# Attention and a snake MLP in one kernel: w_out's last row blocks ahead of v, two requests for late weight pieces, and a new order at the seam of the first two tiles

## The chip, the cores and the metric

One core of a Trainium2 chip runs the whole kernel in one launch. The metric is the device time of one execution in microseconds, the median of several runs. A profile of one further execution shows what each engine did: TensorE (PE; its weight loads are PEld), VectorE (DVE), ScalarE (ACT), GpSimd (POOL), SyncE (SP, which here only issues transfers) and the 16 DMA engines.

## The reference

```python
# q, k, v: 8 batches x 8 heads x 576 rows x 64, f32
q_s = exp(q - max(q, axis=-1));  q_s /= sum(q_s, axis=-1)      # over the 64 columns of a row
k_s = exp(k - max(k, axis=2));   k_s /= sum(k_s, axis=2)       # over the 576 rows
kv   = einsum('bhsd,bhse->bhde', k_s, v)                       # 64 x 64 per head
attn = einsum('bhsd,bhde->bhse', q_s, kv)
x = attn.transpose(0, 2, 1, 3).reshape(4608, 512)
h = x @ w_in                                                   # 512 -> 2048
s = sin(alpha * h)
g = h + s * s / alpha
out = g @ w_out                                                # 2048 -> 512, f32
```

## The kernel before

**Tiles.** The 4608 tokens are nine tiles of 512. For each tile the first product is 16 slots (`ni`) of 128 columns of w_in. A slot is four matmuls of 128x512 (`mm_h`, L275 to L284), one for each chunk of 128 of the 512 inputs, taken in the order 0, 2, 1, 3 (`KO`). ScalarE takes the sine out of PSUM (`sine`, L286), one of ScalarE, GpSimd and VectorE squares it, VectorE combines it with h into g in bf16 (`combine`, L297). The second product is, for each of four blocks of 128 tokens (called m or j), 16 matmuls over the row blocks `ni` of w_out (`mm_o`, L301); its accumulator is copied out of PSUM and stored by two transfers (`evac_o`, L311).

**Attention.** exp of q and k on ScalarE, the row sums and the norm of q on VectorE, v cast to bf16 with a column of ones beside it, so that k's sum falls out of the same product. For batches 0 and 1, `wide_mm(b, ii)` (L178) multiplies k and v for one half of the heads with 18 matmuls, and `wide_norm` (L187) scales the result into `kvw`; `attn_x` (L232) multiplies it with q transposed, and copies put the result into `xT`: half 0 gives the chunks 0 and 2, half 1 the chunks 1 and 3. `ii` is the half throughout.

**Order.** The schedule is written by hand: each engine runs its instructions in the order of the program and waits where one needs another's result. Each of two queues carries loads: SP's (`nc.sync`) takes q, k, v and the stores; GpSimd's takes w_in and w_out, whose requests cast from f32 to bf16 on the way.

**The start.** Batch 0's attention is done first, with w_in coming in pieces (L358 to L363, the last of 512 columns, slots 12 to 15) and w_out's row blocks 0 to 7 behind it (L364). Tile 0's slots run at L478; the dictionary `late` (L476) issues loads after certain slots: q of batch 1 (`load_q1`, L460), w_out's blocks 8 to 11 after slot 8 and 12 and 13 after slot 10, k and v of batch 1 after slot 12 (`load_kv1`, L468). Row blocks 14 and 15 come as f32 on SP's queue into two buffers (`late_w`, L488) behind batch 1's v, and are cast at L543 by GpSimd and ScalarE. Behind them on that queue are `q8` (the ninth row of each group of q for batches 0 and 1, L491) and batch 2's q, k and v.

**The seam of tiles 0 and 1.** Tile 0's second product is a generator of 64 matmuls (`o_quad`, L439): four runs of 16, each over four row blocks of w_out and all four m. The main program takes some of them at a time (`take(os, n)`) between the steps of batch 1's attention: 42, then the first set of transposes of q, 9, the second set, 1, the first wide kv, 3, the first half of attention, 1, the second wide kv, the first products of tile 1's slots 0 and 1 (chunks 0 and 2), the second half of attention, and the last 8. Each accumulator is evacuated as soon as its last product is issued. The four accumulators are in the PSUM buffers "b", "b", "l", "l", and the slots of tile 1 take these over again as they are listed in `BANKS`.

Before tile 1's first sine, ScalarE has exp of `q8` (L545) and a small sine (L551) by which the Sin table is loaded. Tile 1's second product (`o_stream`, L591) takes its first two blocks of tokens up to `ni` 13 each before the last two `ni` of both.

Of the kernel before, what the change touches and what calls it, by code (L numbers as in the profile page):

```python
# [15 lines left out]
F32 = mybir.dt.float32  # L16
BF16 = mybir.dt.bfloat16
AX = mybir.ActivationFunctionType
# [5 lines left out]
def kernel(  # L24
# [14 lines left out]
    nc = tc.nc  # L39
# [7 lines left out]
    nN = d_ff // 128  # L47
    MF = 512
# [12 lines left out]
    spool = ctx.enter_context(tc.tile_pool(name="spool", bufs=4))  # L61
# [6 lines left out]
    xT = singles.tile([128, 4, NX], BF16, name="xT")  # L68
    q8 = singles.tile([128, 4, 2, D], F32, name="q8")
    win = singles.tile([128, 4, d_ff], BF16, name="win")  # L70
    wout = singles.tile([128, nN, dm], BF16, name="wout")
# [11 lines left out]
    wout_v = moe_w_out.rearrange("(no ni) d -> ni no d", ni=128)  # L83
# [23 lines left out]
    def load_win(c0, c1, cc=slice(0, 4)):  # L107
        nc.gpsimd.dma_start(out=win[:, cc, c0:c1], in_=win_v[:, cc, c0:c1])  # L108

    def load_wout(n0, n1):  # L110
        nc.gpsimd.dma_start(out=wout[:, n0:n1, :], in_=wout_v[:, n0:n1, :])
# [43 lines left out]
    def norm_q8():  # L155

        qe = A["qe", 1][:, J - 2:J].rearrange("p b (i d) -> p b i d", i=4)
        qs = small.tile([128, 2, 4], F32, name="qs8")
        nc.vector.tensor_reduce(qs, qe, axis=AXL.X, op=ALU.add)
        nc.vector.reciprocal(qs, qs)  # L160
        return lambda: nc.vector.tensor_tensor(qe, qe, qs.unsqueeze(3).to_broadcast([128, 2, 4, D]), op=ALU.mult)
# [101 lines left out]
    G = {}  # L263

    HP = {}
    BANKS = {0: "aabbkllaabbkllaa", 1: "aakbbllaabbllaab", 2: "aabbopaabbopaabb"}

    def bank(kind):

        if kind == "k":  # L270
            return ps_k.tile([128, 2, MF], F32, name="kvp", tag="a")[:, 0]
        pool = {"a": lambda: ps_h[0], "b": lambda: ps_h[1], "l": lambda: ps_l, "o": lambda: ps_o[0], "p": lambda: ps_o[1]}[kind]()
        return pool.tile([128, MF], F32, name={"l": "lp", "o": "op", "p": "op"}.get(kind, "hp"), tag=kind)

    def mm_h(t, ni, k0=0, k1=4):  # L275

        if ni == 0 and k0 == 0:
            G[t] = gpool.tile([128, nN, MF], BF16, name="g")
        hp = HP[t, ni] if k0 else bank(BANKS.get(t, 3 * "aabb" + "abba")[ni])
        HP[t, ni] = hp  # L280
        for k in range(k0, k1):
            nc.tensor.matmul(hp, win[:, KO[k], ni * 128:(ni + 1) * 128],  # L282
                             xT[:, KO[k], t * MF % NX:t * MF % NX + MF], start=(k == 0), stop=(k == 3))
        return hp  # L284

    def sine(t, ni, hp, sq):  # L286
        s = spool.tile([128, MF], F32, name="s")
        nc.scalar.activation(s, hp, AX.Sin, scale=alpha_sb[:, ni:ni + 1])  # L288
        if sq == "A":
            nc.scalar.activation(s, s, AX.Square)  # L290
        elif sq == "P":
            nc.gpsimd.tensor_tensor(s, s, s, op=ALU.mult)  # L292
        else:
            nc.vector.tensor_tensor(s, s, s, op=ALU.mult)
        return s
# [9 lines left out]
    def place(blk):  # L305

        if blk < 2 * (J - 1):
            return blk // (J - 1), blk % (J - 1)
        return (blk - 2 * (J - 1), J - 1) if blk < 2 * J else (blk // J, blk % J)

    def evac_o(t, j, acc, eng, cols=None, queues=None):  # L311
        cols = cols or slice(0, dm)
        o = opool.tile([128, dm], F32, name="o")
        eng(o[:, cols], acc)  # L314
        for hf in range(2):
            bb, jj = place(t * BPT + 2 * j + hf)
            (queues or (nc.sync, nc.sync))[hf].dma_start(out=out_v[bb, jj][:, cols],
                                                         in_=o[64 * hf:64 * hf + 64, cols])


    ACT_CP, DVE_CP, GP_CP = nc.scalar.copy, nc.vector.tensor_copy, nc.gpsimd.tensor_copy
# [13 lines left out]
    zero = singles.tile([128, 1], F32, name="zero")  # L335
# [24 lines left out]
    load_win(0, 512, slice(1, 4, 2))  # L360
    for c in range(2, 6):
        load_win(256 * c, 256 * c + 256)
    load_win(1536, 2048)  # L363
    for c in range(2):  # L364
        load_wout(4 * c, 4 * c + 4)

# [62 lines left out]
        mm_h(0, ni, ki, ki + 1)  # L429

    def h_slot(t, ni, sq, lag):
        hp = mm_h(t, ni, 2 if ni < (4, 2, 0)[min(t, 2)] else 0)
        lag.append((t, ni, hp, sine(t, ni, hp, sq)))

    def flush(lag, keep):
# [3 lines left out]
    def o_quad(t, accs, engs):  # L439

        R = range(4)
        by_m, by_n = [(n, m) for m in R for n in R], [(n, m) for n in R for m in R]
        orders = [by_m, by_n, by_n, by_n[:8] + [(n, m) for m in R for n in (2, 3)]]
        for c in R:
            for n, m in orders[c]:
                mm_o(t, m, 4 * c + n, accs[m])
                if c == 3 and n == 3:
                    evac_o(t, m, accs[m], engs[m])
                yield

    def take(it, n=1000):
        for _ in range(n):
            if next(it, 0) == 0:
                return
# [4 lines left out]
    with ES:  # L459
        def load_q1(ii):  # L460
            if ii == 0:
                staged["q", 1] = stage.tile([128, 4, J, D], F32, name="st_q", tag="st")
            st = staged["q", 1]
            DVE_CP(st[:, ii, 0, 0:1], zero)
            nc.sync.dma_start(out=st[:, ii::2, 0:8].rearrange("p i j d -> p i (j d)"),
                              in_=src_view(q, 1)[:, ii::2, 0:8 * D])

        def load_kv1():  # L468
            for n in "kv":
                staged[n, 1] = stage.tile([128, 4, J, D], F32, name=f"st_{n}", tag="st")  # L470
            for n, t, ii, j0, j1 in (("k", k, 0, 0, J), ("v", v, 0, 0, J), ("k", k, 1, 0, J),
                                     ("v", v, 1, 0, 5), ("v", v, 1, 5, J)):
                nc.sync.dma_start(out=staged[n, 1][:, ii::2, j0:j1].rearrange("p i j d -> p i (j d)"),
                                  in_=src_view(t, 1)[:, ii::2, j0 * D:j1 * D])

        late = {6: lambda: load_q1(0), 8: lambda: load_wout(8, 12), 10: lambda: load_wout(12, 14),  # L476
                12: lambda: (load_q1(1), load_kv1())}
        for ni in range(nN):  # L478
            h_slot(0, ni, "DPPAPPAPPAAPPAPD"[ni], lag)
            flush(lag, 1)  # L480
            if ni in late:
                late[ni]()
        flush(lag, 0)

        accs = [bank(kind) for kind in "bbll"]
        os = o_quad(0, accs, [DVE_CP, ACT_CP, DVE_CP, DVE_CP])

        late_w = [spool.tile([128, MF], F32, name="s") for _ in range(2)]  # L488
        for n in range(2):
            nc.sync.dma_start(out=late_w[n], in_=wout_v[:, 14 + n])  # L490
        for b in range(2):  # L491
            nc.sync.dma_start(out=q8[:, :, b], in_=src_view(q, b)[:, :, 8 * D:J * D])
        load_batch(2)
# [1 line left out]
        def cast_v1(ii):  # L495
            vv = vb[1].rearrange("p j (i c) -> p i j c", i=4)
            for j0, j1, eng in (((0, 5, ACT_CP), (5, 9, GP_CP)), ((0, 5, GP_CP), (5, 9, DVE_CP)))[ii]:
                eng(vv[:, 2 * ii:2 * ii + 2, j0:j1, 0:D], staged["v", 1][:, ii::2, j0:j1])
# [29 lines left out]
        exp_half("k", 1, 1)  # L528
        take(os, 9)
        transpose_q1(1, DVE_CP)  # L530
        take(os, 1)
        wide_mm(1, 0)
        wide_norm(1, 0)
        take(os, 3)
        cast_v1(1)
        xa = [bank("a") for _ in range(2)]
        attn_x(1, 0, 0, 8, xa)
        for x in range(2):
            (ACT_CP, DVE_CP)[x](xT[:, 2 * x, MF:2 * MF], xa[x])
        take(os, 1)  # L540
        wide_mm(1, 1)
        wide_norm(1, 1)
        for n, eng in ((0, GP_CP), (1, ACT_CP)):  # L543
            eng(wout[:, 14 + n], late_w[n])
        exp_to(A["qe", 1][:, J - 2:J], q8)  # L545
        for ni, ki in ((0, 0), (1, 0), (0, 1), (1, 1)):
            mm_h(1, ni, ki, ki + 1)
        xb = ps_k.tile([128, 2, MF], F32, name="kvp", tag="a")
        attn_x(1, 1, 0, 8, [xb[:, x] for x in range(2)])
        DVE_CP(xT[:, 1:4:2, MF:2 * MF], xb)  # L550
        nc.scalar.activation(zero, zero, AX.Sin)  # L551
        take(os)
        scale_q8 = norm_q8()
        load("q", q, 3)
        load("k", k, 3)
# [35 lines left out]
    def o_stream(t, eng=DVE_CP):  # L591
        order = [(j, ni) for j in range(4) for ni in range(nN)]
        if t == 1:
            order = [(j, ni) for n0, n1 in ((0, nN - 2), (nN - 2, nN)) for j in range(2) for ni in range(n0, n1)] + order[2 * nN:]
        acc = {}
        for j, ni in order:
            if ni == 0:
                acc[j] = bank("b" if t == 1 and j == 0 else "op"[j % 2])
            mm_o(t, j, ni, acc[j])
            if ni == nN - 1:  # L600
                evac_o(t, j, acc[j], eng)
            yield
# [4 lines left out]
    os = o_stream(1)  # L607
# [55 lines left out]
    for t in range(3, nT):  # L663
        b = t + 1 if t + 1 < B else None
        os = o_stream(t - 1)
# [9 lines left out]
        for ni in range(nN):  # L675
            hp = mm_h(t, ni)
# [20 lines left out]
            s = sine(t, ni, hp, "A")  # L697
# [41 lines left out]
```

## Time and profile before

| | |
|---|---|
| median of 3 runs | 281.84 us (281.73 to 281.9) |
| the profiled execution | 283.14 us, its span 281.3 us |
| granted TensorE clock in it | 0.999 |
| TensorE without a matmul, of the span | 12.9 us: 5.7 before 12.8 us, 3.6 after 270 us |
| tile 0's slots | 15.6 to 28.0 us |
| tile 0's second product, with batch 1's attention in it | 28.0 to 46.4 us |
| tile 1's slots | 46.4 to 59.7 us |
| batch 1's v, first half / last piece | landed by 39.4 / 42.4 us |
| loads and stores of the whole run | 46.06 MB, mean 164 GB/s over the span |

The span is the time from the first to the last instruction that the profile records; the time of a run has something around it. The busy time of a transfer request is from its issue to its landing; idle time of an engine is put down to what ended it.

### The profile page before, as it was taken

The numbers are of one execution on the slowest core, as the hardware profiler recorded it, in microseconds if no ns is written. First come the engines' busy times: TensorE is split into PE (matmuls) and PEld (weight loads), VectorE is DVE, ScalarE is ACT, GpSimd is POOL, SyncE is SP. The second block draws the span as 40 slices with busy tenths as digits, with TensorE's granted clock in tenths as the row PEclk, the third lists the DMA queues.
The fourth block names the chain that finished last, engine by engine and source line by source line (L and its number), as shares of the span: only waits on it lengthen the run. The fifth ranks groups of instructions, "written<-read, shape, count | busy, mean of one in ns | idle before, by whom it ended". The sixth has DMA issues, their size and how long they took to land.

```text
span 281.3 us, 4775 instructions
## 1 busy us (share of the span) xinstructions
PE 268.4 (95%) x1814; PEld 124.2 (44%) x1843; DVE 187.1 (67%) x279; ACT 224.2 (80%) x321; POOL 80.2 (28%) x75
## 2 busy tenths in 40 slices
PE   3899999999999999999999999999999999999994
PEld 1434454444444444444444444444444444444443
DVE  2968867999878767766776677577775555555422
ACT  4799457999588999899989998999877777777400
POOL 2959112678667450215011500350000000000000
PEclk9999999999999999999999999999999999999999
DMA  7999999795699039811981199125011111111143
GB/s 258 299 185 224 276 385 401 266 356 198 156 245 379 3 76 294 336 37 43 328 332 37 40 267 384 37 51 123 10 30 37 37 40 37 38 42 44 41 100 75
DMA packets 39607, 46.06 MB, mean 164 GB/s; under 512 B 17040, under 2 KB 22944, under 8 KB 39584
## 3 DMA queue, kind: packets, MB, share of 16 engines
q1 hardware_dynamic: 33952, 41.11, 46.1%
q0 software_dynamic: 5472, 4.52, 9.8%
q8 instruction: 14, 0.23, 0.3%
q10 hardware_dynamic: 160, 0.13, 0.2%
q14 instruction: 9, 0.07, 0.1%
HBM read 36.71 MB, written 9.44 MB: 164 GB/s over the span
## 4 chain that ended last, share of the span: by engine, by line
PE 87%; DMA 8%; POOL 2%; issue 1%; ACT 0%; SPq 0%; DVE 0%
PE hp L282 38%; PE op L302 37%; DMA wout<-in_moe_w_out_dram 4%; PE hp L302 2%; DMA win<-in_moe_w_in_dram 2%; PE lp L282 2%; DMA st_k<-in_k_dram 2%; PE kvp L173 2%; PE lp L302 1%; PE op L282 1%; PE op L709 1%; PE hp L237 1%; POOL s L292 1%; PE xp L237 1%; PE kvp L282 1%
## 5 line engine op out<-in xcount | busy, mean ns | idle before, releaser
L298 DVE SCALAR_TENSOR_TENSOR g<-s,inva_sb,hp 128x512 bf16<-128x512 f32 x129 | 95.1, 745 | 58.9 <-ACT s L290 53.3
L282 PE MATMUL hp<-xT,win 128*128 128x512 bf16 x508 | 128.8, 379 | 0.8 <-DMA win<-in_moe_w_in_dram 0.4
L302 PE MATMUL op<-wout,g 128*128 128x512 bf16 x463 | 117.6, 379 | 1.7 <-issue 1.3
L288 ACT ACTIVATE s<-hp,alpha_sb 128x512 f32<-128x512 f32 x129 | 87.0, 684 | 21.8 <-PE hp L282 20.3
L282 PEld LDWEIGHTS <-win 128*128 128x128 bf16 x576 | 55.6, 98 | 68.4 <-DMA win<-in_moe_w_in_dram 1.8
L302 PEld LDWEIGHTS <-g 128*128 128x128 bf16 x560 | 53.4, 98 | 65.4 <-issue 2.9
L290 ACT ACTIVATE s<-s 128x512 f32<-128x512 f32 x112 | 70.7, 632 | 3.6
L292 POOL TENSOR_TENSOR s<-s 128x512 f32<-128x512 f32 x28 | 29.5, 1066 | 17.8 <-ACT s L288 17.7
L152 POOL TENSOR_TENSOR qn<-qe,qs 128x1152 bf16<-128x1152 bf16 x11 | 23.2, 2128 | 30.7 <-DVE qs L146 26.3
L314 DVE COPY o<-op 128x512 f32<-128x512 f32 (+2 forms) x32 | 21.1, 660 | 9.7 <-PE op L302 7.4
L137 POOL CAST vb<-st_v 128x1152 bf16<-128x1152 f32 x12 | 14.4, 1228 | 44.5 <-DMA st_v<-in_v_dram 44.2
L118 ACT ACTIVATE qe<-st_q 128x1152 bf16<-128x1152 f32 (+2 forms) x18 | 17.7, 1026 | 6.3 <-DMA st_q<-in_q_dram 6.1
L118 ACT ACTIVATE ke<-st_k 128x1152 bf16<-128x1152 f32 x16 | 17.9, 1153 | 2.6 <-DMA st_k<-in_k_dram 2.6
L145 DVE TENSOR_REDUCE qs<-qe 128x36 f32<-128x2304 bf16 x5 | 12.8, 2552 | 8.3 <-ACT qe L118 8.3
L302 PE MATMUL hp<-wout,g 128*128 128x512 bf16 x45 | 12.0, 379 | 0.5 <-DMA wout<-in_moe_w_out_dram 0.3
L118 ACT ACT_TABLE_LOAD x7 | 9.0, 1283 | 0.8 <-PEq L723 0.7
L302 PE MATMUL lp<-wout,g 128*128 128x512 bf16 x32 | 9.2, 379 | 0.1
L369 PE MATMUL warm<-st_q,ident 128*128 128x512 f32 (+1 forms) x6 | 4.1, 806 | 4.7 <-DMA st_q<-in_q_dram 4.7
L282 PE MATMUL lp<-xT,win 128*128 128x512 bf16 x32 | 7.7, 379 | 0.4 <-DMA win<-in_moe_w_in_dram 0.4
L250 DVE CAST xT<-xp 128x1024 bf16<-128x1024 f32 (+1 forms) x7 | 7.4, 1065 | 0.0
L298 DVE SCALAR_TENSOR_TENSOR g<-s,inva_sb,lp 128x512 bf16<-128x512 f32 x8 | 5.7, 739 | 0.4 <-POOL s L292 0.4
L108 POOL DMA_DIRECT2D win<-in_moe_w_in_dram x8 | 5.9, 772 | 0.0
(98 smaller groups left out, 137.2 us busy)
## 6 DMA issues: line engine op xcount, KB each, us to landing
out_dram<-o SPq DMA_DIRECT2D x70, 128.0 KB, 2.3
st_q<-in_q_dram SPq DMA_DIRECT2D x6, 1152.0 KB, 6.3
st_k<-in_k_dram SPq DMA_DIRECT2D x6, 1152.0 KB, 9.1
st_v<-in_v_dram SPq DMA_DIRECT2D x6, 1152.0 KB, 11.3
st_k<-in_k_dram SPq DMA_DIRECT2D x4, 576.0 KB, 8.3
st_q<-in_q_dram SPq DMA_DIRECT2D x4, 512.0 KB, 6.2
wout<-in_moe_w_out_dram POOLq DMA_DIRECT2D x3, 512.0 KB, 13.7
win<-in_moe_w_in_dram POOLq DMA_DIRECT2D x5, 256.0 KB, 7.9
```

Of the source, the lines that this page charges most:

```text
L118: nc.scalar.activation(dst[:, :, ii * 128:(ii + 1) * 128].rearrange("p j (x d) -> p x j d", x=2), src[:, ii::2], AX.Exp)
L137: engs[ii](vv[:, 2 * ii:2 * ii + 2, :, 0:D], staged["v", b][:, ii::2])
L145: nc.vector.tensor_reduce(qs, A["qe", b].rearrange("p j (i d) -> p j i d", i=4), axis=AXL.X, op=ALU.add)
L152: engs[ii % len(engs)].tensor_tensor(qn[:, ii, 0:j1].rearrange("p j (x d) -> p j x d", x=2), qe[:, ii], part.unsqueeze(3).to_broadcast([12 ...
L250: eng(xT[:, c, d0:d0 + m - n], xp[..., n:m])
L282: nc.tensor.matmul(hp, win[:, KO[k], ni * 128:(ni + 1) * 128], xT[:, KO[k], t * MF % NX:t * MF % NX + MF], start=(k == 0), stop=(k == 3))
L288: nc.scalar.activation(s, hp, AX.Sin, scale=alpha_sb[:, ni:ni + 1])
L290: nc.scalar.activation(s, s, AX.Square)
L292: nc.gpsimd.tensor_tensor(s, s, s, op=ALU.mult)
L298: nc.vector.scalar_tensor_tensor(G[t][:, ni], in0=s, scalar=inva_sb[:, ni:ni + 1], in1=hp, op0=ALU.mult, op1=ALU.add)
L302: nc.tensor.matmul(acc, G[t][:, ni, j * 128:(j + 1) * 128], wout[:, ni, :], start=(ni == 0), stop=(ni == nN - 1))
L314: eng(o[:, cols], acc)
```

## The change

- w_in's last piece is asked for in two requests, chunks 0 and 2, then chunks 1 and 3. Tile 0's slots 12 and 13 begin together with the products of the chunks 0 and 2. A table `BEGUN` tells for each tile which slots have two products already.
- w_out's row blocks 8 to 11 are asked for in two requests, after slots 8 and 10. Blocks 12 to 15 follow in two requests after slot 14, on GpSimd's queue; the f32 buffers and their casts are gone.
- At the seam, tile 0's second product is taken in other portions: 42, 9, 3, 4, 2, 3 and 1. The last run ends accumulator 0 two products after its first eight and takes the others in turn. The second wide kv stands ahead of the last four products. Accumulator 0 is evacuated by ScalarE where its last product is issued, the others after all 64, and after the first two products of tile 1's slot 3.
- The small sine stands ahead of the copies of attention's second half; these are one on VectorE and one on ScalarE, where VectorE made both in one. The cast of v's second half stands behind the copies of attention's first half.
- Tile 1's second product takes its first two blocks of tokens up to `ni` 11.

```diff
+    BEGUN = {0: {ni: 2 for ni in (0, 1, 2, 3, 12, 13)}, 1: {0: 2, 1: 2, 3: 2}}
...
-    load_win(1536, 2048)
+    for r in range(2):
+        load_win(1536, 2048, slice(r, 4, 2))
...
-        hp = mm_h(t, ni, 2 if ni < (4, 2, 0)[min(t, 2)] else 0)
+        hp = mm_h(t, ni, BEGUN.get(t, {}).get(ni, 0))
...
-        orders = [by_m, by_n, by_n, by_n[:8] + [(n, m) for m in R for n in (2, 3)]]
+        orders = [by_m, by_n, by_n, by_n[:8] + [(2, 0), (3, 0)] + [(n, m) for n in (2, 3) for m in (1, 2, 3)]]
...
-                if c == 3 and n == 3:
+                if c == 3 and n == 3 and engs[m]:
...
-        late = {6: lambda: load_q1(0), 8: lambda: load_wout(8, 12), 10: lambda: load_wout(12, 14),
-                12: lambda: (load_q1(1), load_kv1())}
+        late = {6: lambda: load_q1(0), 8: lambda: load_wout(8, 10), 10: lambda: load_wout(10, 12),
+                12: lambda: (load_q1(1), load_kv1()), 14: lambda: (load_wout(12, 14), load_wout(14, 16))}
         for ni in range(nN):
+            for n in (12, 13) if ni == 12 else ():
+                mm_h(0, n, 0, 2)
...
-        os = o_quad(0, accs, [DVE_CP, ACT_CP, DVE_CP, DVE_CP])
-
-        late_w = [spool.tile([128, MF], F32, name="s") for _ in range(2)]
-        for n in range(2):
-            nc.sync.dma_start(out=late_w[n], in_=wout_v[:, 14 + n])
+        os = o_quad(0, accs, [ACT_CP, None, None, None])
+
...
         take(os, 9)
         transpose_q1(1, DVE_CP)
-        take(os, 1)
+        take(os, 3)
         wide_mm(1, 0)
         wide_norm(1, 0)
-        take(os, 3)
-        cast_v1(1)
+        take(os, 4)
         xa = [bank("a") for _ in range(2)]
         attn_x(1, 0, 0, 8, xa)
         for x in range(2):
             (ACT_CP, DVE_CP)[x](xT[:, 2 * x, MF:2 * MF], xa[x])
-        take(os, 1)
+        cast_v1(1)
+        take(os, 2)
+        for ni, ki in ((0, 0), (1, 0), (0, 1)):
+            mm_h(1, ni, ki, ki + 1)
         wide_mm(1, 1)
         wide_norm(1, 1)
-        for n, eng in ((0, GP_CP), (1, ACT_CP)):
-            eng(wout[:, 14 + n], late_w[n])
         exp_to(A["qe", 1][:, J - 2:J], q8)
-        for ni, ki in ((0, 0), (1, 0), (0, 1), (1, 1)):
-            mm_h(1, ni, ki, ki + 1)
+        nc.scalar.activation(zero, zero, AX.Sin)
+        mm_h(1, 1, 1, 2)
+        take(os, 3)
         xb = ps_k.tile([128, 2, MF], F32, name="kvp", tag="a")
         attn_x(1, 1, 0, 8, [xb[:, x] for x in range(2)])
-        DVE_CP(xT[:, 1:4:2, MF:2 * MF], xb)
-        nc.scalar.activation(zero, zero, AX.Sin)
+        for x in range(2):
+            (DVE_CP, ACT_CP)[x](xT[:, 2 * x + 1, MF:2 * MF], xb[:, x])
         take(os)
+        mm_h(1, 3, 0, 2)
+        for m, eng in ((1, ACT_CP), (2, DVE_CP), (3, DVE_CP)):
+            evac_o(0, m, accs[m], eng)
...
-            order = [(j, ni) for n0, n1 in ((0, nN - 2), (nN - 2, nN)) for j in range(2) for ni in range(n0, n1)] + order[2 * nN:]
+            order = [(j, ni) for n0, n1 in ((0, 12), (12, nN)) for j in range(2) for ni in range(n0, n1)] + order[2 * nN:]
```

## The prediction

> **What bounds the kernel now.** I read the page's shares and its chain that ended last, then TensorE's timeline from 12 to 75 us, ScalarE's and VectorE's over the same stretch, the DMA issues with their landings, and the busy times by window.
>
> ```profile
> PE 268.4 (95%) x1814; PEld 124.2 (44%) x1843; DVE 187.1 (67%) x279; ACT 224.2 (80%) x321; POOL 80.2 (28%) x75
> PE 87%; DMA 8%; POOL 2%; issue 1%; ACT 0%; SPq 0%; DVE 0%
> ```
>
> TensorE is the bound. A full product (128x512) starts every 0.216 us (8 in 1.73). Of the 12.9 us without a matmul, 5.7 lie in the first 12.8 us and 3.6 in the last 11.3; the stretch that the change touches has little to give. What it has is seen in TensorE's timeline (start, length, line, what; in brackets the idle time before it):
>
> ```profile
> 24.55 1.90 PE L282 MATMUL lp<-xT,win 128*128 128x512 bf16 x8 [0.39 <-DMA win<-in_moe_w_in_dram]
> ...
> 35.39 0.38 PE L302 MATMUL hp<-wout,g 128*128 128x512 bf16 x1 [0.30 <-DMA wout<-in_moe_w_out_dram]
> ...
> 40.69 0.68 PE L184 MATMUL kvp<-vb,ke 64*128 64x130 bf16 x18
> 41.53 0.38 PE L302 MATMUL hp<-wout,g 128*128 128x512 bf16 x1 [0.16 <-issue]
> ...
> 42.10 0.41 PE L237 MATMUL hp<-qT,kvw 64*64 64x512 bf16 x4
> ...
> 42.77 0.69 PE L184 MATMUL kvp<-vb,ke 64*128 64x130 bf16 x18
> 43.38 1.04 PE L282 MATMUL hp<-xT,win 128*128 128x512 bf16 x4
> 44.35 0.41 PE L237 MATMUL kvp<-qT,kvw 64*64 64x512 bf16 x4
> ```
>
> The two DMA waits cost 0.39 and, by starts (34.92 expected, 35.39 seen), 0.47 us. From 40.4 to 46.4 the starts lie some 0.6 us further apart in all than their work needs. So at most about 1.5 us can be won here. Tile 1's slot 0 goes on at 46.43, with 60 products of the slots left.
>
> Batch 1's part runs on ScalarE like this (same columns):
>
> ```profile
> 37.75 1.17 ACT L118 ACTIVATE ke<-st_k 128x1152 bf16<-128x1152 f32 x1 [1.70 <-DMA st_k<-in_k_dram]
> 39.42 0.74 ACT L498 CAST vb<-st_v 128x640 bf16<-128x640 f32 x1 [0.50 <-DMA st_v<-in_v_dram]
> 40.85 1.17 ACT L118 ACTIVATE ke<-st_k 128x1152 bf16<-128x1152 f32 x1 [0.70 <-DMA st_k<-in_k_dram]
> ...
> 44.86 0.83 ACT L118 ACTIVATE qe<-q 128x256 bf16<-128x256 f32 x2 [0.57 <-DMA q<-in_q_dram]
> 45.71 1.28 ACT L551 ACT_TABLE_LOAD   x1
> 47.00 0.20 ACT L551 ACTIVATE zero<-zero 128x1 f32<-128x1 f32 x1
> 47.11 0.57 ACT L314 COPY o<-hp 128x512 f32<-128x512 f32 x1
> ```
>
> Each step begins where a transfer ends: k's first half lands at 37.7, v's first half at 39.4, k's second at 40.8, the q8 rows at 44.9. v's last piece lands at 42.4 (VectorE's cast begins there). Before W0, the start of the first wide kv at 40.69, the cast of v ended at 40.16. The transfers are the second bound of this stretch, and the windows show the DMA engines full (columns: window, length, busy of PE, PEld, DVE, ACT, POOL, clock, DMA share, GB/s):
>
> ```profile
> 24.00:25.00 1.00, 0.61 (x4) 0.22 (x4) 0.75 (x2) 0.97 (x3) 1.00 (x2) 1.00 1.25 207
> 33.00:34.00 1.00, 1.00 (x6) 0.47 (x5) 0.97 (x2) 0.00 (x0) 0.00 (x0) 1.00 1.11 307
> 37.00:38.00 1.00, 1.00 (x13) 0.65 (x11) 0.93 (x3) 0.25 (x1) 0.00 (x0) 1.00 1.04 401
> ```
>
> With GpSimd's queue alone (casting requests) they write some 205 GB/s, with SP's alone some 400, and between these when both have work.
>
> **The change part by part.**
>
> w_in's last piece in two. Slots 12 and 13 begin with the chunks 0 and 2, four products (0.86 us) that need only the first half. TensorE reaches slot 12 at 24.16; half the piece (256 KB) at 205 GB/s is 1.3 us, so the first half is there by 23.2 and the second at 24.55, when it is needed at 25.02. The 0.39 us goes. One more issue on GpSimd (0.77 us, 13.6 before the w_out pieces) delays only requests that stand behind others for 13.7 and 16.7 us. What is late next is w_out's rows 4 to 7: landed at 14.4 + 16.7 = 31.1, wanted at 31.08 instead of 31.47. I take 0.08 lost.
>
> w_out's rows 8 to 11 in two requests. Both go out where the old two did (24.5 and 25.3). Rows 8 and 9 then land near the middle of 31.1 and 35.35, at 33.2, and are wanted at 34.6; rows 10 and 11 at 35.35, wanted at 36.3. The 0.47 us goes. TensorE reaches product 42 at 36.76 instead of 37.54, 0.78 us ahead.
>
> Rows 12 to 15 at slot 14. GpSimd ends its last square at 29.64, so the two requests go out until 31.2, into a queue that was still busy with rows 8 to 11 until 35.35. Rows 12 and 13 landed at 38.2 before; I leave that, wanted at 38.5. Rows 14 and 15 are 256 KB in bf16: 256 KB / 205 GB/s = 1.26 us of all DMA time, new ahead of v. Before, they went as f32 behind v on SP's queue. How much of the 1.26 falls before v's first half depends on how the two queues share. Between 31.1 and 35.35 GpSimd's queue did 512 KB, 2.52 us of work in 4.25 (59%); between 35.35 and 38.2 at most 1.26 in 2.85 (44%). At 59% v's first half lands 1.26 late, at 44% 0.94 (its last 1.2 us of work then goes at 56%); with SP's queue wholly first, 0. I take 1.26, by the mean of the two (53%), and 0 as the other end. All that follows on SP's queue until q8 is 1.26 late; q8 itself stays at 44.9, as the f32 rows no longer stand before it.
>
> On this the Trainium skill has a rule (DMA: Bandwidth & Descriptors, Queues, rings and completion order): each DMA engine goes round the queues that have work, a packet of each in turn. Taken as halves that would make v 1.2 late instead of 1.26, and the sum 0.06 smaller; the trace's 59 and 44% lie on both sides of it.
>
> Removed: two f32 loads on SP, and the casts of row blocks 14 and 15 (0.62 us on GpSimd, 0.62 on ScalarE, both with idle time of 0.5 us before them). Worth nothing on the path: q8's landing ends last.
>
> The new order from W0. TensorE would arrive after 42 + 9 + 3 products and two sets of transposes (0.45 each) at 40.25. v's first half at 39.42 + 1.26 = 40.68 and ScalarE's cast of 0.74 make W0 = 41.42; here the 0.78 us ahead is lost, with 0.4 more. The 18 kv matmuls take 0.61, four products 0.86: attention's first half at 42.9. k's second exp is over at 40.85 + 1.26 + 1.17 = 43.28. Then ScalarE has the evacuation of accumulator 0, put ahead of chunk 0's copy: 0.57 + 0.59 less 0.05 of overlap, 44.4. Before, that copy had begun 0.46 after attention's start. Covered by only two products, the first slot products of tile 1 wait for it until 44.4 (they would come at 43.7). Three of them: 45.05. The second wide kv needs v's last piece, cast by 42.42 + 1.26 + 0.43 = 44.1: no wait. 0.61 + four products 0.86: attention's second half at 46.5 (its norm took 1.35 from the kv's start, 46.4). VectorE's copy of chunk 1 begins 0.46 later and takes 0.69: 47.67. ScalarE copies chunk 3 behind exp of q8 and the Sin table: 47.11 + 0.59 = 47.70. Cover is now one product and two, 0.65 us, where it was eight (1.73). So slot 0 goes on at 47.7, with 58 products of the slots left: before, that point was 46.43 + 2 x 0.216 = 46.86. **Lost: 0.84 us.**
>
> Behind it. Accumulators 1 to 3 are evacuated after this; ScalarE's one (0.5 us) stands before its first sine, which starts at about 48.4 instead of 47.58, as late as TensorE. ScalarE was without a gap until 61.1, so it keeps that distance; buffers came free 0.24 us ahead of TensorE at the tightest (slot 9, wanted at 53.3, combine over at 53.06), and both shift by the same. Tile 1's second part with 12 instead of 14 in its first run: block 14 is wanted two products sooner (0.43 us), with its combine over at 62.03 and the product at 66.0 before; 3.5 us of cover stay. From 60 us on TensorE is idle 1 us in 100, and no transfer ends a wait of it, so the shift lasts to the end.
>
> **Sum.** 281.3 + 0.84 = 282.14 of span. The median shown is 0.54 above that span (281.84; this profiled run took 283.14 in all), so 282.68, said as 282.7.
>
> **The rivals.**
>
> A, the forecast, 0.47: 282.7; its own range 282.2 (the 44% share, d = 0.94 late, and 0.2 of copy time less) to 283.1.
>
> B, v a little late, 0.28: v half a microsecond behind and q8 earlier, as SP's ring has no f32 rows. W0 = 40.7, slot 0 at 46.95: 281.9. For it: the 44% row, and 16 engines that do not end together. Against: DMA share over 1 throughout.
>
> C, v in its place, 0.15, the other side: SP's queue is served first until v is in. W0 = 40.25, attention at 41.7. If the evacuation does not hold chunk 0's copy, it ends at 42.8, and slot 0 goes on at 46.1: 281.1; with the evacuation first, 46.4: 281.4. It needs q8 by 44.2 as well, since the Sin table and chunk 3's copy follow it by 2.8. It is faster from a v under 0.3 us late. Against: GpSimd's queue had 44 to 59% of the engines while SP's was full.
>
> D, w_out's rows 14 and 15 come late themselves, 0.10: with a small share they land after 42.5, where product 57 wants them. Landing at 43.4 gives 283.3. Rows 12 and 13 landed 12.9 us after issue; 30.4 + 12.9 = 43.3 speaks for it, a full queue at 25.3 against it.
>
> **How the numbers follow.** This kernel's runs tell 0.2% (0.56 us) from no change. Slower: A without its low end (0.45) and D (0.10), 0.55. Faster: most of C, 0.13. Same: B, A's and C's edges, 0.32. The range 281.3 to 283.3 leaves out C's lower half and half of D, some 0.14.
>
> **What would show it.** Right: no wait for w_in near 24.5 or for w_out near 35; a wait before the first wide kv, which starts near 41.4 after a v that lands after 40.3; tile 1's first slot products held by ScalarE's copy behind the evacuation; ScalarE's first sine of tile 1 near 48.4. Wrong: v's first half by 39.7, or q8 before 44.2, or a first sine before 47.6. Then the path I call lost is not, and the kernel is level or faster.

## The result, and the profile after

| | before | after |
|---|---|---|
| median | 281.87 us (6 runs, 281.73 to 282.48) | 283.81 us (6 runs, 283.3 to 284.47) |
| ratio | | 1.0064, 95% interval 1.0047 to 1.0081 |
| span of the profiled execution | 281.3 us | 281.6 us |
| time of the profiled execution | 283.14 us | 283.35 us |

The changed kernel is slower by 1.9 us. The two profiles differ by only 0.3 us of span. Both are right: the profiled execution of after lies at the fast end of its runs, and that of before is 1.3 us above its median. The time around the span is nearly the same everywhere, 1.7 to 1.9 us in every run of this case, so an ordinary execution of before has a span of about 280.1 us, not 281.3. The experiments begin with such an execution.

The page after, the same two lines as shown of before:

```profile
PE 272.0 (97%) x1843; PEld 125.0 (44%) x1843; DVE 186.0 (66%) x278; ACT 224.2 (80%) x322; POOL 81.9 (29%) x77
PE 83%; DMA 5%; ACT 4%; DVE 3%; POOL 1%; issue 1%; SPq 0%; ACTq 0%
```

TensorE is still the bound, but ScalarE and VectorE now have a part in the chain that ended last. TensorE's timeline after, at the places shown of before (start, length, line, what, idle time before it):

```profile
23.57 1.89 PE L283 MATMUL lp<-xT,win 128*128 128x512 bf16 x8
...
34.79 0.59 PE L303 MATMUL hp<-wout,g 128*128 128x512 bf16 x2
...
39.14 0.59 PE L303 MATMUL hp<-wout,g 128*128 128x512 bf16 x2
39.95 0.69 PE L184 MATMUL kvp<-vb,ke 64*128 64x130 bf16 x18 [0.21 <-ACT vb L499]
...
42.10 0.38 PE L303 MATMUL lp<-wout,g 128*128 128x512 bf16 x1
43.03 0.81 PE L283 MATMUL hp<-xT,win 128*128 128x512 bf16 x3 [0.55 <-ACT xT L539]
43.77 0.69 PE L184 MATMUL kvp<-vb,ke 64*128 64x130 bf16 x18
...
45.35 0.41 PE L237 MATMUL kvp<-qT,kvw 64*64 64x512 bf16 x4
...
45.92 1.01 PE L283 MATMUL hp<-xT,win 128*128 128x512 bf16 x3
47.18 0.81 PE L283 MATMUL hp<-xT,win 128*128 128x512 bf16 x3 [0.24 <-ACT xT L553]
```

No wait for w_in or w_out is left, and three new ones stand at the seam: for v's cast (0.38 us by starts, 39.57 to 39.95), for chunk 0 (0.72, 42.31 to 43.03) and for the chunks 1 and 3 (0.61 us by starts: with no wait slot 0's products of these two chunks would begin at 46.35 and 46.57, and the second one begins at 47.18). The bracket shows less than the starts do, since the row of one product is 0.38 us long while the next product can start 0.22 us after it. ScalarE's timeline after shows what they wait for:

```profile
36.26 1.16 ACT L118 ACTIVATE ke<-st_k 128x1152 bf16<-128x1152 f32 x1 [1.48 <-DMA st_k<-in_k_dram]
39.16 0.73 ACT L499 CAST vb<-st_v 128x640 bf16<-128x640 f32 x1 [1.73 <-DMA st_v<-in_v_dram]
40.85 1.16 ACT L118 ACTIVATE ke<-st_k 128x1152 bf16<-128x1152 f32 x1 [0.96 <-DMA st_k<-in_k_dram]
41.92 0.57 ACT L315 COPY o<-hp 128x512 f32<-128x512 f32 x1
42.39 0.59 ACT L539 CAST xT<-hp 128x512 bf16<-128x512 f32 x1
43.52 0.83 ACT L118 ACTIVATE qe<-q 128x256 bf16<-128x256 f32 x2 [0.54 <-DMA q<-in_q_dram]
44.36 1.28 ACT L547 ACT_TABLE_LOAD   x1
...
46.54 0.58 ACT L553 CAST xT<-kvp 128x512 bf16<-128x512 f32 x1 [0.68 <-DVE xT L553]
```

VectorE's copy of chunk 1, just before that last row:

```profile
45.82 0.69 DVE L553 CAST xT<-kvp 128x512 bf16<-128x512 f32 x1 [0.69 <-PE kvp L237]
```

v's first half ends a wait of 1.73 us at 39.16; the evacuation at 41.92 stands ahead of chunk 0's copy at 42.39; chunk 3's copy waits for VectorE's copy of chunk 1, not for the Sin table, which was in by 45.9.

### The profile page after: what moved, and what is told of

Its sections match the earlier page's. It is cut to its first block, busy times and chain, and to the rows that moved or that the text cites. A ratio compares the mean times of both kernels' runs of the same rounds, so it can differ in the third digit from the quotient of the medians.

```text
span 281.6 us, 4800 instructions
## 1 busy us (share of the span) xinstructions
PE 272.0 (97%) x1843; PEld 125.0 (44%) x1843; DVE 186.0 (66%) x278; ACT 224.2 (80%) x322; POOL 81.9 (29%) x77
## 3 DMA queue, kind: packets, MB, share of 16 engines
q0 software_dynamic: 5776, 4.79, 10.2%
## 4 chain that ended last, share of the span: by engine, by line
PE 83%; DMA 5%; ACT 4%; DVE 3%; POOL 1%; issue 1%; SPq 0%; ACTq 0%
PE op L303 37%; PE hp L283 37%; DMA st_k<-in_k_dram 4%; ACT s L289 2%; PE kvp L173 2%; PE hp L303 1%; DMA st_q<-in_q_dram 1%; PE op L283 1%; PE op L714 1%; PE lp L283 1%; POOL s L293 1%; DVE qs L385 1%; DVE qn L387 1%; PE hp L237 1%; PE xp L237 1%
## 5 line engine op out<-in xcount | busy, mean ns | idle before, releaser
L303 PE MATMUL op<-wout,g 128*128 128x512 bf16 x480 | 120.4, 379 | 0.0
L145 DVE TENSOR_REDUCE qs<-qe 128x36 f32<-128x2304 bf16 x5 | 12.8, 2550 | 8.7 <-ACT qe L118 8.7
L303 PE MATMUL hp<-wout,g 128*128 128x512 bf16 x48 | 13.0, 379 | 0.0
L371 PE MATMUL warm<-st_q,ident 128*128 128x512 f32 (+1 forms) x6 | 4.8, 938 | 4.6 <-DMA st_q<-in_q_dram 4.6
L108 POOL DMA_DIRECT2D win<-in_moe_w_in_dram x9 | 6.6, 788 | 0.0
```

The source lines that it names most:

```text
L145: nc.vector.tensor_reduce(qs, A["qe", b].rearrange("p j (i d) -> p j i d", i=4), axis=AXL.X, op=ALU.add)
L303: nc.tensor.matmul(acc, G[t][:, ni, j * 128:(j + 1) * 128], wout[:, ni, :], start=(ni == 0), stop=(ni == nN - 1))
```

## The experiments

The experiments were made in three groups, and the kernel before was run again beside each; its medians were 282.35 us (12 runs), 282.14 (25) and 281.99 (21). A ratio is that of the means of the runs to before's in the same group, so it can differ a little from the quotient of the medians.

### A second execution of before

The kernel is unchanged.

> The kernel before, unchanged, for a second profiled execution. Theory 1 (the profile that the prediction was built on was an unlike execution: 283.14 us against a median of 281.87, with three waits for weights of 0.36, 0.39 and 0.47 us in TensorE's row): a span near 280.1, TensorE without waits for w_in and w_out, tile 1's slot 0 going on at 45.1 to 45.4 instead of 46.43. Rival (that execution was an ordinary one, and the time around the span is what varies): a span of 281.3 with the same three waits.

Measured: 281.81 us (one run), span 280.0. TensorE's timeline:

```profile
23.60 1.89 PE L282 MATMUL lp<-xT,win 128*128 128x512 bf16 x8
...
34.82 0.59 PE L302 MATMUL hp<-wout,g 128*128 128x512 bf16 x2
...
39.38 0.68 PE L184 MATMUL kvp<-vb,ke 64*128 64x130 bf16 x18
...
42.07 1.04 PE L282 MATMUL hp<-xT,win 128*128 128x512 bf16 x4
...
45.11 1.03 PE L282 MATMUL hp<-xT,win 128*128 128x512 bf16 x4
```

There is no bracket at all: between 12.8 and 62 us TensorE waits for nothing that the profile shows. Slot 0 goes on at 45.11, 1.32 us ahead of the execution that the prediction read. The three waits for weights in that one (0.36 at 15.2, 0.39 at 24.2, 0.47 at 34.9, in all 1.22 us) are about the 1.3 us by which it was longer than the median. In this ordinary execution ScalarE begins the cast of v's first half at

```profile
37.63 0.74 ACT L498 CAST vb<-st_v 128x640 bf16<-128x640 f32 x1 [0.24 <-DMA st_v<-in_v_dram]
```

against 39.16 after: by this pair of traces v is 1.5 us late in the changed kernel. From issue to landing v's first half takes 8.9 us here and 10.5 after. The pair alone would not be enough, since in the long execution of before it took 10.4 us with nothing new ahead of it; the times of the runs below decide, and the landings in all traces are compared in the section on the prediction.

### The seam's copies, in the changed kernel

Accumulator 0's evacuation behind the copies of attention's first half:

```diff
-        os = o_quad(0, accs, [ACT_CP, None, None, None])
+        os = o_quad(0, accs, [None] * 4)
...
             (ACT_CP, DVE_CP)[x](xT[:, 2 * x, MF:2 * MF], xa[x])
+        evac_o(0, 0, accs[0], ACT_CP)
```

> The changed kernel with accumulator 0's evacuation put behind the copies of attention's first half on ScalarE. Theory 1 (the seam's copies are what is lost): TensorE's wait for chunk 0 (0.72 us from 42.31 to 43.03) shrinks to some 0.2, and the time falls by 0.5 us, to 283.3. Theory 2 (the requests are what is lost: v and k land late, and a gap won ahead of the second wide kv is lost again at it): no more than 0.1 us.

Measured: 283.93 us (282.9 to 284.17), ratio 1.0046 (1.003 to 1.0063). Then also two PSUM tiles for attention's second half:

```diff
-        xb = ps_k.tile([128, 2, MF], F32, name="kvp", tag="a")
-        attn_x(1, 1, 0, 8, [xb[:, x] for x in range(2)])
+        xb = [bank("k"), bank("b")]
+        attn_x(1, 1, 0, 8, xb)
...
-        mm_h(1, 3, 0, 2)
```

> As the run before, and attention's second half goes into two PSUM tiles instead of the two banks of one, so that ScalarE's copy of chunk 3 needn't wait for VectorE's of chunk 1; slot 3's first two products go back behind slot 2. Theory 1: both waits (0.72 and 0.61 us) shrink to 0.2 or less, time 282.6 to 282.9. Theory 2: 283.7.

Measured: 283.92 us (282.88 to 284.62), ratio 1.0051 (1.0032 to 1.007). Chunk 0's wait did shrink, to 0.3 us by starts in both, but in both traces v's cast begins at 40.1 and the first wide kv only at 40.9. Neither is told apart from the changed kernel's 1.0064. So chunk 0's copy is not what decides, and the wait for v is the longest one in both traces.

### All requests of the change, the old order at the seam

```diff
-        take(os, 3)
+        take(os, 1)
         wide_mm(1, 0)
         wide_norm(1, 0)
-        take(os, 4)
+        take(os, 3)
+        cast_v1(1)
...
```

and so on back to the order of before, without the f32 buffers and their casts.

> All requests of the changed kernel (w_in's last piece and w_out's blocks 8 to 11 in two, 12 to 15 after slot 14, no f32 buffers), with the order of before at the seam (portions 42, 9, 1, 3, 1 and 8, evacuations as each accumulator ends, VectorE copying the chunks 1 and 3, blocks up to 13 first in tile 1). Theory 1: the seam's waits go, 281.6 to 282.0, level with before. Theory 2: 283.2 to 283.8, as the changed kernel.

Measured: 283.81 us (282.94 to 284.52), ratio 1.0049 (1.0031 to 1.0068). The old order does not bring the time back. At the seam its TensorE waits at one place, longer there than in the trace after:

```profile
40.83 0.69 PE L184 MATMUL kvp<-vb,ke 64*128 64x130 bf16 x18 [1.20 <-ACT vb L499]
```

So the theory of the copies falls as the main cause; the requests make the loss.

### Which request

Blocks 14 and 15 alone, in the kernel before:

```diff
         late = {6: lambda: load_q1(0), 8: lambda: load_wout(8, 12), 10: lambda: load_wout(12, 14),
-                12: lambda: (load_q1(1), load_kv1())}
+                12: lambda: (load_q1(1), load_kv1()), 14: lambda: load_wout(14, 16)}
...
-        late_w = [spool.tile([128, MF], F32, name="s") for _ in range(2)]
...
-            eng(wout[:, 14 + n], late_w[n])
```

> The kernel before with one part of the change: w_out's row blocks 14 and 15 are asked for on GpSimd's queue after slot 14, and the f32 buffers and their casts are gone; all else, the order at the seam too, as before. Theory 2 (these 512 KB of f32 go ahead of batch 1's k and v and hold them back): v's first half lands 1.3 to 2.5 us later than in the ordinary execution of before (37.6), the first wide kv starts at 40.7 or later instead of 39.4, time 283.2 to 284. Rival (it is the later issue of blocks 12 and 13, or the split pieces): level with before.

Measured: 283.98 us (283.49 to 284.35), ratio 1.0063 (1.0038 to 1.0087): the whole loss, from one part of the change. Its TensorE and ScalarE:

```profile
40.87 0.69 PE L184 MATMUL kvp<-vb,ke 64*128 64x130 bf16 x18 [0.53 <-ACT vb L495]
```

```profile
40.09 0.73 ACT L495 CAST vb<-st_v 128x640 bf16<-128x640 f32 x1 [0.88 <-DMA st_v<-in_v_dram]
```

This execution also had a wait of 0.8 us for w_in near 15, which moves all of it; from issue to landing v's first half took 10.7 us against 8.9.

Blocks 12 and 13 alone:

```diff
-        late = {6: lambda: load_q1(0), 8: lambda: load_wout(8, 12), 10: lambda: load_wout(12, 14),
-                12: lambda: (load_q1(1), load_kv1())}
+        late = {6: lambda: load_q1(0), 8: lambda: load_wout(8, 12),
+                12: lambda: (load_q1(1), load_kv1()), 14: lambda: load_wout(12, 14)}
```

> The kernel before with one part of the change: blocks 12 and 13 asked for after slot 14 instead of slot 10; blocks 14 and 15 stay on SP's queue behind v. Theory 2: level with before within 0.2%, since the same bytes stand ahead of v as long as GpSimd's queue is still busy with blocks 8 to 11. Rival: v waits for them, or product 48 does, and the time is 0.5 us or more above before.

Measured: 282.15 us (281.82 to 283.83), ratio 1.001 (0.9994 to 1.0026): no loss that the interval can tell.

The two splits alone, with the slots 12 and 13 begun together:

```diff
-    load_win(1536, 2048)
+    for r in range(2):
+        load_win(1536, 2048, slice(r, 4, 2))
...
-        late = {6: lambda: load_q1(0), 8: lambda: load_wout(8, 12), 10: lambda: load_wout(12, 14),
+        late = {6: lambda: load_q1(0), 8: lambda: load_wout(8, 10), 10: lambda: (load_wout(10, 12), load_wout(12, 14)),
...
```

> The kernel before with the two splits alone: w_in's last piece in two requests with slots 12 and 13 begun together, and w_out's blocks 8 to 11 in two, 12 and 13 right behind them. By the ordinary execution of before, which shows no wait for weights from 13 to 42 us: level with before. By the prediction's working: 0.8 us faster.

Measured: 282.47 us (282.13 to 283.18), ratio 1.0013 (1.0001 to 1.0024). The splits win nothing; if anything they cost a little. The trace of this run has a wait of 0.38 us of TensorE at 29.1 for VectorE's combine, which the trace after does not have.

### The bytes or the queue

Half the dose, block 14 alone:

```diff
+                12: lambda: (load_q1(1), load_kv1()), 14: lambda: load_wout(14, 15)}
...
+        late_w = spool.tile([128, MF], F32, name="s")
+        nc.sync.dma_start(out=late_w, in_=wout_v[:, 15])
...
+        ACT_CP(wout[:, 15], late_w)
```

> Half the dose: the kernel before with row block 14 alone on GpSimd's queue after slot 14; block 15 stays f32 on SP's queue behind v. Theory 2 (bytes ahead of v): about half of the 1.8 us that both blocks cost, 282.8 to 283.2. Rival (any request of GpSimd beside k and v breaks SP's stream): nearly the whole, 283.6 or more.

Measured: 282.72 us (282.24 to 284.2), ratio 1.002 (1.0002 to 1.0038), 0.73 us above before's median where both blocks cost 1.84: a part of the loss, not the whole, and just under what was expected.

The same bytes ahead of k and v on SP's own queue, without a cast on the way:

```diff
+        late_w = [singles.tile([128, MF], F32, name=f"late_w{n}") for n in range(2)]
+
+        def load_late_w():
+            for n in range(2):
+                nc.sync.dma_start(out=late_w[n], in_=wout_v[:, 14 + n])
...
-                12: lambda: (load_q1(1), load_kv1())}
+                12: lambda: (load_q1(1), load_late_w(), load_kv1())}
...
-        late_w = [spool.tile([128, MF], F32, name="s") for _ in range(2)]
-        for n in range(2):
-            nc.sync.dma_start(out=late_w[n], in_=wout_v[:, 14 + n])
```

> The kernel before with its two f32 loads of the blocks 14 and 15 moved on SP's own queue ahead of batch 1's k and v (into buffers of their own). Theory 2: the same bytes ahead of v on the other queue without a cast, v 1.3 us late or more, 283.2 to 284. Rival (it is GpSimd's queue or its casting requests that slow SP's): 282.5 or less.

Measured: 283.74 us (283.42 to 284.21), ratio 1.0052 (1.0033 to 1.007).

```profile
41.09 0.69 PE L184 MATMUL kvp<-vb,ke 64*128 64x130 bf16 x18 [0.92 <-ACT vb L501]
```

The loss comes with either queue: it is the place of the 512 KB of f32 ahead of v, not GpSimd's queue or its casts.

The blocks on GpSimd's queue behind v's first half:

```diff
         cast_v1(0)
+        load_wout(14, 16)
```

> The kernel before with the blocks 14 and 15 on GpSimd's queue, but asked for behind its first cast of batch 1's v; no f32 buffers, no casts of them. Theory 2: v's first half is on time (37.6 to 38.5) and the first wide kv starts by 39.7; k's second half and v's last pieces now share with these blocks, so 0.3 to 1.0 us are lost at the second wide kv: 282.3 to 283. Rival (the queue, not the place): 283.5 or more.

Measured: 288.82 us (287.14 to 289.17), ratio 1.0217 (1.0179 to 1.0254).

```profile
39.27 0.68 PE L184 MATMUL kvp<-vb,ke 64*128 64x130 bf16 x18
...
47.51 1.86 PE L302 MATMUL hp<-wout,g 128*128 128x512 bf16 x4 [4.16 <-DMA wout<-in_moe_w_out_dram]
```

The first wide kv is on time (39.27 against 39.38 in the ordinary execution), with GpSimd's queue in use: again the place and not the queue. The expectation was wrong on what comes next: the request goes out at 38.87 and lands 8.6 us later; until almost 43 us SP's queue alone moves data, and why GpSimd's begins so late was not studied. TensorE waits 4.16 us for the blocks, and what follows runs at half its clock for a while (in the last section).

### The new order by itself

Blocks 14 and 15 asked for behind v, 12 and 13 in their place in tile 0's second product:

```diff
-        nc.tensor.matmul(acc, G[t][:, ni, j * 128:(j + 1) * 128], wout[:, ni, :],
+        nc.tensor.matmul(acc, G[t][:, ni, j * 128:(j + 1) * 128], wout[:, ni - 2 if t == 0 and ni > 13 else ni, :],
...
-                12: lambda: (load_q1(1), load_kv1()), 14: lambda: (load_wout(12, 14), load_wout(14, 16))}
+                12: lambda: (load_q1(1), load_kv1()), 14: lambda: load_wout(12, 14)}
...
         cast_v1(1)
+        load_wout(14, 16)
```

> The changed kernel, but blocks 14 and 15 are asked for only behind batch 1's v (after GpSimd's second cast of v), and tile 0's second product uses the blocks 12 and 13 in their place, so that part of the computation is changed. It shows the new order at the seam with v on time. Theory 2: the first wide kv starts within 0.3 us of before's, and the new order costs 0.6 us or less by itself: time 281.9 to 282.9. Theory 1 (the order's own waits for copies): the waits for the chunks 0 and 3 stay at 0.7 and 0.6 us, time 283 or more.

Measured: 282.89 us (282.73 to 284.34), ratio 1.0031 (1.0016 to 1.0047). With v on time the new order costs 0.8 us. In this sum are the two splits and the later request of the blocks 12 and 13, which were 1.0013 and 1.001 alone, so the order's own share may be smaller. The first wide kv began at 40.36, not within 0.3 us of the ordinary execution's 39.38 as expected: 0.50 us is a wait for w_in that this execution had, and 0.43 the two products more that stand ahead. It waits at the same two places as the changed kernel:

```profile
43.18 0.81 PE L283 MATMUL hp<-xT,win 128*128 128x512 bf16 x3 [0.28 <-ACT xT L539]
...
47.32 0.81 PE L283 MATMUL hp<-xT,win 128*128 128x512 bf16 x3 [0.24 <-ACT xT L554]
```

The same with both edits of the copies:

> As the run of the new order with v on time (the blocks 12 and 13 in place of 14 and 15 in tile 0's second product, so part of the computation is changed), with accumulator 0's evacuation behind the copies of attention's first half, and attention's second half in two PSUM tiles. If the 0.8 us of the new order are its two waits for copies, TensorE's waits for the chunks 0 and 3 fall to 0.2 and the time to 282.0 to 282.4; if they are something else, it stays at 282.9.

Measured: 282.89 us (282.67 to 283.57), ratio 1.0024 (1.0009 to 1.004). No gain beyond the interval:

```profile
42.74 0.81 PE L283 MATMUL hp<-xT,win 128*128 128x512 bf16 x3
...
46.26 1.02 PE L283 MATMUL hp<-xT,win 128*128 128x512 bf16 x4 [0.47 <-DVE xT L555]
```

The two copies of attention's second half now run side by side on ScalarE and VectorE (begun at 45.55 and 45.52), and TensorE still waits for them. A copy is done 1.2 us after attention starts, and behind attention stands one product here, one and two of slot 3 in the change, eight in the order of before. This edit took the two products of slot 3 away, 0.43 us of cover, so it does not tell how much of the 0.8 us the wait of one copy for the other makes; that stays open. That eight products behind attention would bring it back is argued from the order of before, not shown.

## Why the prediction was wrong

The direction was right, and so was the first link of the mechanism: the two blocks make v late, and TensorE waits for its cast. The time was outside the range. The step that failed is the gain that the sum sets against the loss, "The 0.39 us goes" and "The 0.47 us goes", and with it the base, "The median shown is 0.54 above that span". The loss of 0.84 us is a loss of 1.62 at the seam less 0.78 us won at two waits for weights. These waits belong to the one execution that was read; an ordinary one does not have them, so nothing is won, and 281.84 + 1.62 is 283.46, against 283.81 measured. The remaining 0.35 us is not fully placed; the copy of chunk 3, below, is the part of it that a trace shows.

From the side of the span it is the same mistake. The 0.54 was the difference of a median and of an execution that was 1.3 us longer than it, where the time around the span is 1.7 to 1.9 us. The sign of that was in the numbers shown (283.14 us for this execution, 281.84 for the median), and so was its cause, three waits for weights of 1.22 us in all. That the forecast span of 282.14 lies near the median of the changed kernel's six spans (282.0, from 281.5 to 282.7) is luck in part: it still holds the third of those waits (0.36 us at 15.2), and it prices the copy of chunk 3 too low.

Point by point:

- **The splits.** "The 0.39 us goes", "The 0.47 us goes": they are gone in the trace after, and in the ordinary execution of before as well. By themselves the splits give 1.0013. The term measured nothing instead of 0.78 us.
- **Blocks 12 and 13.** Left as they were, and so it is: 1.001 with nothing else changed.
- **Blocks 14 and 15 ahead of v.** Predicted 1.26 us late for v's first half (256 KB at 205 GB/s are 1.28); measured 1.5 in the trace after (39.16 against 37.63). From issue to landing it took 10.5 to 11.5 us, mean 11.0, in the five traces with both blocks on GpSimd's queue early, and 8.8 to 10.4, mean 9.5, in the seven without either block ahead of v; the 10.4 is that of the long execution. Right in kind, and near in size. The windows show the share of the two queues (columns as in the prediction; first the ordinary execution of before, then after):

```profile
36.00:38.00 2.00, 2.00 (x17) 1.13 (x16) 1.93 (x3) 1.54 (x2) 0.34 (x1) 1.00 1.04 405
```

```profile
36.00:38.00 2.00, 2.00 (x17) 1.13 (x15) 1.93 (x4) 1.16 (x1) 0.00 (x0) 1.00 1.12 295
```

  At 405 GB/s SP's queue has the engines to itself; at 295 both queues write, where half of each queue's rate by itself (400 and 205) gives 302. In these 2 us of the trace after, SP's queue moved 191 packets and GpSimd's 193, with 58.9% and 53.5% of the engines' time, close to the 53% that the prediction took; in the ordinary execution of before SP's moved all 409. The Trainium skill's rule of packets in turn (DMA: Bandwidth & Descriptors, Queues, rings and completion order) agrees with these counts, as far as the profile's packets are those of the rule. The run with the two blocks on SP's queue shows that the loss does not hang on it.
- **The new order from W0.** The first wide kv was forecast at 41.42 and came at 39.95 in this trace, the fastest but one of six, and at 40.83 to 40.94 in three other traces with the same requests. The wait for v's cast was forecast at 1.17 us (40.25 to 41.42); it was 0.38 in the trace after, and 1.4 and 1.2 in the two traces of the changed kernel with other copies. The wait for chunk 0 behind the evacuation was forecast at 0.7 us and was 0.72. For chunk 3 both price and reason were wrong. From attention's start to the last copy's end the prediction has 1.2 us (46.5 to 47.7), which leaves a wait of 0.2 behind one product and two; it took 1.8 (45.35 to 47.12), and the wait was 0.61. The Sin table was in, and the copy waited for VectorE's. That wait of one copy for the other stands in the program for two copies out of one PSUM tile, and with two tiles the copies ran side by side; the prediction did not look for it.
- **The signs.** Two of the signs of being wrong came true by the clock, v's first half by 39.7 (39.16) and q8 before 44.2 (43.5), and yet the kernel is slower. They were set on the times of the long execution, which ran 1.3 us behind an ordinary one at the seam. Against the ordinary execution v is 1.5 us late and q8 0.4 (43.52 against 43.16), so the time on that path was lost all the same. The first sine came at 47.65, which is 1.8 us after that of the ordinary execution (45.87), where 0.8 was forecast.
- **Behind it.** The shift does last to the end: 1.41 us at 60 us (60.04 against 58.63 in the ordinary execution) and 1.40 at the last tile's products (274.08 against 272.68).
- **How the parts add.** v late costs 1.84 us by itself (1.0063), the new order with v on time 0.8, the two together 1.9. They do not add. The new order puts two more products (0.43 us) ahead of the first wide kv, which can shorten the wait for v; that this is why, and that the rest is such cover too, is argued only.
- **The rivals.** B and C fall with v's landing, 1.5 us late against the ordinary execution. D falls: blocks 14 and 15 took 10.2 us from issue to landing and were in at 40.2, and product 57, which needs them, started at 41.01 without a wait.

## What to carry to other kernels

Hold the profiled execution against the median before anything is worked out from it: where it is longer, its extra waits are in the trace, and a change that removes them wins nothing in the median. Where the DMA engines are full, as here, a load moved ahead of another makes that one late by about its own time on the engines (1.28 us of work, 1.5 us late), and the loss came with either queue, so price it by the consumer of what is pushed back. Bringing a chain's last link forward moves the work that covered its copies out from behind it; count the products that are left.

## What the runs showed of the hardware

- The executions of before lie between 281.62 and 283.4 us. The one long execution traced has three waits for weights, the first for w_in at 15.2 us; a wait at the same place is in the traces of three experiments, of 0.8 us in the run with the blocks 14 and 15 alone and of 0.5 and 0.2 us in the two runs of the new order with v on time. What makes w_in late in some executions was not studied.
- Half of the bytes ahead of v cost less than half by the medians (0.73 us against 1.84); the interval of the half, 1.0002 to 1.0038, does not exclude half of 1.0063. In the ordinary execution of before there is a little slack: GpSimd's cast of v ended at 39.03 and the first wide kv began at 39.38. That this makes a difference is argued only.
- TensorE's clock. In the run with the blocks behind v's first half, the windows (columns as in the prediction, the granted clock behind the busy time of GpSimd) show it halved after the wait of 4.16 us:

```profile
42.00:43.00 1.00, 1.00 (x10) 0.33 (x8) 0.67 (x3) 0.75 (x2) 0.00 (x0) 1.00 1.11 429
47.00:49.00 2.00, 1.49 (x4) 0.56 (x4) 0.44 (x1) 0.00 (x0) 0.00 (x0) 0.50 1.05 412
...
53.00:55.00 2.00, 1.95 (x9) 0.90 (x9) 1.12 (x2) 1.85 (x4) 0.96 (x2) 0.90 0.87 204
```

  TensorE's last product before the wait ended at 43.35; the granted clock was still 1.00 from 46.0 to 46.5 and was 0.58 from 46.5 to 47.0, more than 3 us later. Four products took 1.86 us instead of 1.04 there, and the full clock came back only past 53 us. The waits of up to 1.2 us in the other traces left it at 1.00 (whole-span means of 0.997 or more). The Trainium skill (TensorE: Matmul & The Clock Gate, Part 1: The HAM clock gate) puts the bound at an idle window of about 3.4 us, to which both observations fit.
